# Seven quarter products from chunk 4 on, and a row's scores and values in different chunks

## The chip, the cores and the metric

The kernel runs on one core of a Trainium2 chip. The time is device time in microseconds of one launch, from the median of several runs. TensorE is PE in the views, and its weight loads PEld; VectorE is DVE, ScalarE is ACT, GpSimd is POOL, SyncE is SP. A "q" behind a name (SPq, POOLq) means that engine's queue of DMA issues and waits.

## What is computed

Local attention in two kinds of heads, and behind it a two-layer network on all tokens:

```python
# q, k, v: (8 batches, 8 heads, 576, 64) float32; w_in (512, 2048), w_out (2048, 512)
scores = q @ k.T / 8
# heads 0-3: key in the last 32 positions; heads 4-7: every 4th of the last 128
attn = softmax(where(mask, scores, -1e9))
x = (attn @ v).transpose(0, 2, 1, 3).reshape(4608, 512)
out = maximum(x @ w_in, 0) ** 2 @ w_out
```

The 4608 x 512 result is float32. Inside, the kernel works in float16 and accumulates in float32 in PSUM.

## The kernel before

**Two units.** A *row* is one batch: 576 tokens of attention. A *chunk* is 512 tokens of the network (chunk 0 takes row 0's 576 tokens whole, chunk 1 then has 448). So eight rows feed nine chunks: row b is wanted by chunk b and lies beside chunk b-1 in the program.

**The network.** The first product of a chunk (`mm1_gen`, L285, L264) makes sixteen tiles of 128 hidden units by 512 tokens, with four 512-wide matmuls each. ACT applies the relu from PSUM into `rt` (L249); DVE squares it into `g` (L253). The plain second product (`mm2_gen`, L316, L296) has four tiles of 16 matmuls, 512 wide. Chunks 7 and 8 use a Winograd form instead (`seven_gen`, L408, L401): `g` and `w_out` are cut into 2 x 2 quarters, DVE forms sums of quarters (`sum_g`, L372, for S1 to S4; `sum_w_out`, L359, for T1 to T4), PE makes seven products of quarters with 16 matmuls each, 256 wide, and DVE combines them from PSUM (L446 to L472).

**Attention of a row.** Four score groups (`s_sliding`, L582, twice, and `s_dilated`, L589, twice): PE writes scores into a pair of PSUM banks, ACT takes the exponential into `AT` (L547), DVE multiplies with a 0/1 mask (L549). Then seven groups of values (`av_sliding`, L609, three; `av_dilated`, L624, four): PE multiplies `AT` with `v` and its column of ones, DVE takes the reciprocal of the sum and multiplies (L600, L601). Last come four groups of PE transposes (`x_sliding`, L638; `x_dilated`, L655), which ACT copies into `xT` (L650, L668). `xT` is a ring of four rows; a chunk whose tokens cross the ring's end has each matmul of its first product cut in two (`cut`, L260).

**What sets the order.** Each engine works through its instructions in the order in which the program emits them. The network's generators yield after every half tile of the first product (two matmuls), every two matmuls of the second and every four of the seven, and `pump(n)` (L486) lets them go n steps: the first product has 32 steps, the plain second product 32, the seven 28 in all. Before, each chunk ran 24 steps, then four score groups 4 steps apart, then values and transposes 2 steps apart (L673, L681, L892 on). PSUM has eight banks: four for the network (`bank`), and two pairs for attention (`pair`).

**Loads.** POOL waits with a one-element copy (`see`, L181) until row b's q and k have landed, then issues the loads of row b+1's, copies these into token order (L225) and casts row b's v (L197, L201). SP issues, in this order within a chunk, the DMA transposes of row b+1 into `QKTd` and `QKTp` (two buffers each), the loads of its v, and the chunk's stores.

Of the kernel before, what the change touches and what calls it, by code (L numbers as in the profile page):

```python
# [8 lines left out]
FP16 = mybir.dt.float16  # L9
FP32 = mybir.dt.float32  # L10
# [3 lines left out]
P = 128  # L14
# [3 lines left out]
def kernel(  # L18
# [40 lines left out]
    natp = ctx.enter_context(tc.tile_pool(name="natp", bufs=2))  # L59
# [27 lines left out]
    RING = 4 * S  # L87
# [8 lines left out]
    g = wpool.tile([P, NFF, S], FP16, name="g")  # L96

# [149 lines left out]
    def relu_squared(ph, w, outs, name):  # L247
        rt = osb.tile([P, TOKC], FP16, name=name, tag="rt")
        nc.scalar.activation(rt[:, 0:w], ph[:, 0:w], ACTF.Relu)  # L249
        o = 0  # L250
        for g in outs:
            n = g.shape[1]
            nc.vector.tensor_mul(g, rt[:, o : o + n], rt[:, o : o + n])  # L253
            o += n

    def mm1_tile(name, ffc, t0, t1, outs):
# [16 lines left out]
        relu_squared(ph, w, outs, f"rt{name}")  # L273
        yield

    def mm1_first_gen():

        for f4 in range(0, NFF, 4):
            for t0 in (0, HALF):
                for ffc in range(f4, f4 + 4):  # L280
                    yield from mm1_tile(
                        f"0_{ffc}_{t0}", ffc, t0, t0 + HALF, [g[:, ffc, t0 : t0 + HALF]]
                    )

    def mm1_gen(c, then=None):  # L285
        o = REST if c == 1 else 0
        for ffc in range(NFF):
            yield from mm1_tile(
                f"{c}_{ffc}", ffc, c * TOKC + o, (c + 1) * TOKC, [g[:, ffc, o:TOKC]]
            )  # L290
            if then is not None:
                then(ffc)
# [50 lines left out]
    sums = {}  # L343

    def quarters():

        for i, tag in enumerate(("nd", "nd", "n", "n", "o", "o")):
            shape = {"nd": [P, 36 * D], "n": [P, HH, 9, D], "o": [P, 9, HH, D]}[tag]
            u = natp.tile(shape, FP16, name=f"sum{i}", tag=tag)
            if tag != "nd":  # L350
                u = u.rearrange("p a b d -> p (a b d)")
            sums[("T1", "T2", "T3", "S1", "S2", "S3")[i]] = u[:, 0 : HF * HT].rearrange(
                "p (j t) -> p j t", j=HF
            )
        u = sd.rearrange("p t h x -> p (t h x)").bitcast(FP16)
        for i, name in enumerate(("T4", "S4")):
            sums[name] = u[:, HF * HT * i : HF * HT * (i + 1)].rearrange("p (j t) -> p j t", j=HF)

    def sum_w_out(name, j):  # L359

        f = slice(4 * j, 4 * j + 4)
        b11, b12 = wo[j][:, :, 0:HT], wo[j][:, :, HT:DM]
        b21, b22 = wo[2 + j][:, :, 0:HT], wo[2 + j][:, :, HT:DM]
        a, b = {
            "T1": (b12, b11),
            "T3": (b22, b12),
            "T2": (b22, sums["T1"][:, f, :]),
            "T4": (b21, sums["T2"][:, f, :]),
        }[name]
        nc.vector.tensor_sub(sums[name][:, f, :], a, b)  # L370

    def sum_g(name, j):  # L372

        f, h = slice(4 * j, 4 * j + 4), slice(HF + 4 * j, HF + 4 * j + 4)
        a11, a12 = g[:, f, 0:HT], g[:, h, 0:HT]
        a21, a22 = g[:, f, HT:TOKC], g[:, h, HT:TOKC]
        o = sums[name][:, f, :]
        if name == "S1":
            nc.vector.tensor_add(o, a21, a22)
        elif name == "S3":  # L380
            nc.vector.tensor_sub(o, a11, a21)
        elif name == "S2":
            nc.vector.tensor_sub(o, sums["S1"][:, f, :], a11)
        else:
            nc.vector.tensor_sub(o, a12, sums["S2"][:, f, :])

    def sums_behind(ffc):
        for name, j in {
            8: (("S3", 0),),
            9: (("S3", 1),),  # L390
            12: (("S1", 0),),
            13: (("S2", 0),),
            14: (("S4", 0),),
            15: (("S1", 1), ("S2", 1), ("S4", 1)),
        }.get(ffc, ()):
            sum_g(name, j)

    def product(po, lhs, rhs):
        for t in range(2):
# [6 lines left out]
            yield  # L406

    def seven_gen(c):  # L408
# [6 lines left out]
        def s(name):  # L415
            return lambda j: sums[name][:, j, :]

        def new(name):
            return osb.tile([P, 2, HT], FP32, name=f"{name}{c}", tag=name, bufs=1)
# [8 lines left out]
        def keep(i, k, o):  # L428
            for t in range(2):
                nc.sync.dma_start(out=rows(i, k, t), in_=o[:, t, :])  # L430
# [5 lines left out]

        p1, po = one()
        yield from product(po, a(0, 0), b(0, 0))
        s1 = new("s1")
        nc.scalar.copy(s1, p1)  # L440
        p7, po = one()
        yield from product(po, s("S3"), s("T3"))
        p2, po = one()
        yield from product(po, a(0, 1), b(1, 0))
        c11 = outcome("c11")
        nc.vector.tensor_add(c11, p2, s1)  # L446
        keep(0, 0, c11)
        p6, po = one()
        yield from product(po, s("S2"), s("T2"))
        u2, t7 = new("u2"), new("t7")  # L450
        nc.vector.tensor_add(u2, p6, s1)
        nc.vector.tensor_add(t7, p7, u2)
        p5, po = one()
# [92 lines left out]
    def softmax(u, ps, mask, eng=nc.vector):  # L546
        nc.scalar.activation(AT[:, u, 0:UW], ps[:, :, 0 : UW // 2], ACTF.Exp, scale=scale)  # L547
        if mask is not None:
            eng.tensor_mul(AT[:, u, 0:UW], AT[:, u, 0:UW], mask)  # L549
# [397 lines left out]
```

## Time and profile before

| what | us |
|---|---|
| median of 3 runs (lowest, highest) | 314.33 (313.9, 314.9) |
| the profiled execution | 315.87 |
| its span, from the first to the last instruction | 313.8 |
| PE busy in the span | 299.6 |
| DVE, ACT, POOL busy | 181.7, 167.3, 78.0 |
| first products (L264), 704 matmuls, on the chain that ended last | 39.0% |
| plain second products (L296), 448 matmuls, on that chain | 30.3% |
| seven products (L401), 224 matmuls, on that chain | 7.8% |

The span covers what the profiler recorded of the program; the execution's own time has 2.1 us more around it. Durations are those of one execution. A matmul's recorded duration is longer than the distance to the next one, since matmuls are pipelined, so PE's rate is read from the distance between starts or from the chain's merged pieces, where "x64" stands for that many instructions in a row.

### The profile page before, as it was taken

How to read it: one execution, taken by the hardware profiler on the slowest of the kernel's cores; microseconds unless marked ns; L12 is line 12 of the kernel's file. 1: busy time of each engine (PE TensorE's matmuls, PEld its weight loads, DVE VectorE, ACT ScalarE, POOL GpSimd, SP SyncE). 2: the span in 40 equal slices, each digit the busy share in tenths (PEclk: the TensorE clock that was granted, in tenths of full speed). 3: DMA queues.
4: the chain of work that ended last, by engine and by line, in shares of the span. 5: the costliest groups of instructions: out<-in, count | busy, mean ns of one | idle time of the engine just before them, and what ended most of it. 6: DMA issues, size and time to landing. Idle time of an engine off the chain costs nothing.

```text
span 313.8 us, 6835 instructions
## 1 busy us (share of the span) xinstructions
PE 299.6 (96%) x2724; PEld 183.7 (59%) x2724; DVE 181.7 (58%) x402; ACT 167.3 (53%) x295; POOL 78.0 (25%) x120
## 2 busy tenths in 40 slices
PE   3978999999899999999999999999999999999995
PEld 3647955555455555555579655545554555686584
DVE  6445647736742795396524653475388534854764
ACT  2646856378336753677257724683368336604610
POOL 5483016403523633263340370032000000000000
PEclk9989999999999999999999999999999999999999
DMA  6999989599989999998968992992100110012012
GB/s 118 223 191 214 212 179 216 123 164 256 229 185 202 278 193 188 236 280 172 221 218 193 176 239 75 186 206 101 45 25 1 41 61 36 1 40 96 0 36 100
DMA packets 73951, 46.71 MB, mean 149 GB/s; under 512 B 54528, under 2 KB 68096, under 8 KB 73728
## 3 DMA queue, kind: packets, MB, share of 16 engines
q1 hardware_dynamic: 66384, 32.39, 43.2%
q0 software_dynamic: 7248, 13.63, 24.4%
q8 instruction: 21, 0.34, 0.4%
q10 hardware_dynamic: 288, 0.26, 0.2%
q14 instruction: 10, 0.08, 0.1%
HBM read 39.85 MB, written 16.52 MB: 180 GB/s over the span
## 4 chain that ended last, share of the span: by engine, by line
PE 88%; DMA 7%; POOL 2%; issue 1%; ACT 1%; DVE 0%; POOLq 0%
PE PS L264 39%; PE PS L296 30%; PE PS L401 8%; PE PS L629 3%; DMA wi<-in_moe_w_in_dram 3%; DMA sd<-in_v_dram 2%; DMA n<-in_q_dram 2%; PE PS L615 2%; PE PS L574 1%; PE PS L644 1%; PE PS L560 1%; PE PS L662 1%; ACT AT L547 0%; PE PS L504 0%; PE PS L528 0%
## 5 line engine op out<-in xcount | busy, mean ns | idle before, releaser
L264 PE MATMUL PS<-xT,wi 128*128 128x512 f16 (+3 forms) x704 | 130.3, 343 | 1.8 <-DMA wi<-in_moe_w_in_dram 1.1
L249 ACT ACTIVATE rt<-PS 128x512 f16<-128x512 f32 (+2 forms) x160 | 88.8, 556 | 44.6 <-PE PS L264 40.5
L296 PE MATMUL PS<-wo,g 128*128 128x512 f16 x448 | 112.5, 379 | 0.0
L253 DVE TENSOR_TENSOR g<-rt 128x512 f16<-128x512 f16 (+2 forms) x160 | 69.8, 443 | 72.1 <-ACT rt L249 71.5
L264 PEld LDWEIGHTS <-wi 128*128 128x128 f16 x704 | 78.4, 114 | 46.8 <-DMA wi<-in_moe_w_in_dram 1.2
L296 PEld LDWEIGHTS <-g 128*128 128x128 f16 x448 | 37.3, 97 | 31.4
L547 ACT ACTIVATE AT<-PS 128x576 f16<-128x576 f32 x64 | 38.3, 650 | 8.6 <-PE PS L574 5.7
L306 ACT COPY ot<-PS 128x512 f32<-128x512 f32 x28 | 16.4, 586 | 28.8 <-PE PS L296 28.8
L650 ACT COPY xT<-PS 128x576 f16<-128x576 f16 x16 | 10.2, 639 | 29.4 <-PE PS L644 29.4
L201 POOL CAST vd<-sd 128x512 f16<-128x512 f32 x32 | 20.5, 669 | 14.7 <-DMA sd<-in_v_dram 12.5
L197 POOL CAST vp<-sv 128x512 f16<-128x512 f32 x24 | 16.7, 710 | 27.1 <-DMA sv<-in_v_dram 27.1
L601 DVE TENSOR_TENSOR x_d<-PS,rcp_d 72x512 f16<-72x512 f32 x32 | 22.0, 686 | 1.1
L225 POOL COPY o<-n 128x2304 f16<-128x2304 f16 x6 | 12.6, 2107 | 27.8 <-DMA n<-in_q_dram 27.6
L549 DVE TENSOR_TENSOR AT<-AT,maskd 128x576 f16<-128x576 f16 x28 | 14.6, 539 | 7.0 <-ACT AT L547 5.6
L600 DVE RECIPROCAL rcp_d<-PS 72x8 f32<-72x8 f32 x32 | 6.5, 202 | 20.7 <-PE PS L629 19.6
L629 PEld LDWEIGHTS <-AT 128*128 128x128 f16 x256 | 12.8, 102 | 7.8 <-DVE x_d L601 0.8
L601 DVE TENSOR_TENSOR x_p<-PS,rcp_p 96x512 f16<-96x512 f32 x24 | 16.5, 686 | 0.8
L549 DVE TENSOR_TENSOR AT<-AT,maskp 128x576 f16<-128x576 f16 x28 | 14.3, 524 | 4.0 <-ACT AT L547 2.1
L668 ACT COPY xT<-PS 128x576 f16<-128x576 f16 x16 | 10.2, 640 | 8.8 <-PE PS L662 8.8
L629 PE MATMUL PS<-vd,AT 128*128 128x65 f16 x256 | 14.3, 200 | 0.0
L183 POOL COPY look<-QKTp 1x1 f16<-1x1 f16 x5 | 1.2, 239 | 49.3 <-DMA QKTp<-dp 49.3
L615 PEld LDWEIGHTS <-AT 128*128 128x128 f16 x192 | 9.2, 99 | 6.6 <-issue 1.2
(86 smaller groups left out, 207.9 us busy)
## 6 DMA issues: line engine op xcount, KB each, us to landing
out_dram<-ot SPq DMA_DIRECT2D x27, 256.0 KB, 2.8
sv<-in_v_dram SPq DMA_DIRECT2D x40, 128.0 KB, 4.6
sd<-in_v_dram SPq DMA_DIRECT2D x8, 512.0 KB, 11.4
dp<-o SPq DMA_DIRECT2D x12, 288.0 KB, 3.7
sd<-in_v_dram SPq DMA_DIRECT2D x8, 288.0 KB
wo<-in_moe_w_out_dram POOLq DMA_DIRECT2D x4, 512.0 KB, 13.6
out_dram<-c SPq DMA_DIRECT2D x14, 128.0 KB, 1.8
n<-in_k_dram POOLq DMA_DIRECT2D x6, 288.0 KB, 6.1
```

Source lines behind the costliest of these rows:

```text
L197: nc.gpsimd.tensor_copy(vp[b % 2][:, m : m + 2, :, 0:D], sv[:, m : m + 2, :, :])
L201: nc.gpsimd.tensor_copy(vd[b % 2][:, t, c : c + 2, :, 0:D], sd[:, t, :, D * c : D * (c + 2)].rearrange("p h (c d) -> p c h d", d=D),)
L249: nc.scalar.activation(rt[:, 0:w], ph[:, 0:w], ACTF.Relu)
L253: nc.vector.tensor_mul(g, rt[:, o : o + n], rt[:, o : o + n])
L264: nc.tensor.matmul(ph[:, a:b], w_in_of(dmk, ffc), xT[:, dmk, x : x + b - a], start=(dmk == 0 and a == 0), stop=(dmk == NDM - 1 and b == w),)
L296: nc.tensor.matmul(po, g[:, ffc, o + t * P : o + (t + 1) * P], w_out_of(ffc), start=(ffc == 0), stop=(ffc == NFF - 1),)
L306: nc.scalar.copy(ot, po)
L401: nc.tensor.matmul(po[t], lhs(j)[:, t * P : (t + 1) * P], rhs(j), start=j == 0, stop=j == HF - 1)
L547: nc.scalar.activation(AT[:, u, 0:UW], ps[:, :, 0 : UW // 2], ACTF.Exp, scale=scale)
L549: eng.tensor_mul(AT[:, u, 0:UW], AT[:, u, 0:UW], mask)
L601: nc.vector.tensor_tensor(out=x[0:w], in0=pv[:, :, :, 0:D], in1=rcp[0:w].unsqueeze(3).to_broadcast([w, 2, HH, D]), op=ALU.mult,)
L629: nc.tensor.matmul(pav[:, e, h * (D + 2) : h * (D + 2) + D + 1], AT[:, 4 + 2 * a + t, off : off + P], vd[b % 2][:, t, 2 * a + e, h, 0 : D ...
```

## The change

- Chunks 4, 5 and 6 use the seven products as well. The sums of `w_out` are made once, in chunk 2. S4 takes S3's place after product 7, and its two sums come behind product 2.
- Rows 2 and 3 keep their places. Row 4 has its scores at steps 2 to 20 of chunk 3 and its values at 24 to 44; row 5 its scores at 47 to 59 of chunk 3 and its values in the first half of chunk 4; rows 6 and 7 have their scores at steps 36 to 54 of chunks 4 and 5, their values at steps 2 to 32 of the chunk after. From row 4 on the transposes use the pair banks too (`wide`).
- Squares are made for two tiles in one DVE instruction, masks for two tiles likewise. A quarter of the result is stored by one DMA.
- The ring `xT` has three rows; `n` and `o` have one buffer each; S1 to S3 and T4 have tiles of their own; the first rows' staging tiles share slots with T1 to T3.
- In the seven, product 4 skips the bank of product 7.

The diff, cut to its core:

```diff
-    natp = ctx.enter_context(tc.tile_pool(name="natp", bufs=2))
+    n1p = ctx.enter_context(tc.tile_pool(name="n1p", bufs=1))
+    natp = ctx.enter_context(tc.tile_pool(name="natp", bufs=1))
...
-    RING = 4 * S
+    RING = 3 * S
...
+    S1, S2, S3 = (wpool.tile([P, NFF // 2, TOKC // 2], FP16, name=f"S{i}") for i in (1, 2, 3))
+    T4 = wpool.tile([P, NFF // 2, TOKC // 2], FP16, name="T4")
...
-        relu_squared(ph, w, outs, f"rt{name}")
-        yield
+        nc.scalar.activation(rt, ph[:, 0:w], ACTF.Relu)
+
+    def new_rt(name):
+        return osb.tile([P, 2, TOKC], FP16, name=f"rt{name}", tag="rt", bufs=3)
...
+        for f2 in range(0, NFF, 2):
+            rt = new_rt(f"{c}_{f2}")
+            for i in range(2):
+                yield from mm1_tile(f2 + i, c * TOKC + o, (c + 1) * TOKC, rt[:, i, o:TOKC])
+                if i == 1:
+                    nc.vector.tensor_mul(g[:, f2 : f2 + 2, o:TOKC], rt[:, :, o:TOKC], rt[:, :, o:TOKC])
+                    if then is not None:
+                        then(f2)
+                yield
...
+    def sum_g(name, j):
+
         f = slice(4 * j, 4 * j + 4)
+        if name == "S3":
+            nc.vector.tensor_sub(S3[:, f, :], a_of(0, 0, j), a_of(1, 0, j))
+        elif name == "S1":
+            nc.vector.tensor_add(S1[:, f, :], a_of(1, 0, j), a_of(1, 1, j))
         elif name == "S2":
+            nc.vector.tensor_sub(S2[:, f, :], S1[:, f, :], a_of(0, 0, j))
         else:
+            nc.vector.tensor_sub(S3[:, f, :], a_of(0, 1, j), S2[:, f, :])
+
+    def sums_behind(f2):
         for name, j in {
             8: (("S3", 0),),
+            10: (("S3", 1),),
+            12: (("S1", 0), ("S2", 0)),
+            14: (("S1", 1), ("S2", 1)),
+        }.get(f2, ()):
             sum_g(name, j)
...
         def keep(i, k, o):
-            for t in range(2):
-                nc.sync.dma_start(out=rows(i, k, t), in_=o[:, t, :])
+            t0 = c * TOKC + HT * i
+            nc.sync.dma_start(
+                out=out[t0 : t0 + HT, HT * k : HT * (k + 1)].rearrange("(t p) m -> p t m", p=P),
+                in_=o,
+            )
...
         yield from product(po, a(0, 1), b(1, 0))
+        for j in range(2):
+            sum_g("S4", j)
         c11 = outcome("c11")
...
+        turn["bank"] += 1
         p4, po = one()
...
+    def softmax(u, tiles, mask):
+
+        n = len(tiles)
+        for i, ps in enumerate(tiles):
+            nc.scalar.activation(
+                AT[:, u + i, 0:UW], ps[:, :, 0 : UW // 2], ACTF.Exp, scale=scale
+            )
         if mask is not None:
+            nc.vector.tensor_mul(
+                AT[:, u : u + n, 0:UW],
+                AT[:, u : u + n, 0:UW],
+                mask.unsqueeze(1).to_broadcast([P, n, UW]),
+            )
...
-        t0 = (b % 4) * S + 288 * half
+        t0 = (b % 3) * S + 288 * half
...
+    def run(*plans, more=()):
+
+
+        todo = list(more)
+        for plan, parts in plans:
+            for w in plan.split():
+                step, *names = w.split(":")
+                todo += [(int(step), parts[n]) for n in names]
+        at = 0
+        for step, part in sorted(todo, key=lambda t: t[0]):
+            pump(step - at)
+            at = max(at, step)
+            part()
+        pump(1000)
...
+    rows_ = {b: row_parts(b, b > 3) for b in range(2, B)}
+    SCORES = "{}:s0 {}:s1 {}:z0 {}:z1"
+    VALUES = "{}:a0 {}:a1 {}:a2 {}:x0 {}:d0 {}:x1 {}:d1 {}:e0 {}:e1 {}:y0 {}:y1"
+    for c in range(1, NTOKC):
+        b = c + 1
...
+        pending.append(moe_gen(c) if c < 4 else moe_seven_gen(c))
+        plans, more = [], []
+        if c < 3:
+            plans.append((SCORES.format(*range(24, 40, 4)), rows_[b]))
+            plans.append((VALUES.format(*range(40, 62, 2)), rows_[b]))
+        if c == 2:
+            it = sum_w_out_gen()
+            more = [(4 + 7 * i, lambda it=it: next(it)) for i in range(8)]
+        if c == 3:
+            plans.append((SCORES.format(2, 8, 14, 20), rows_[b]))
+            plans.append((VALUES.format(*range(24, 46, 2)), rows_[b]))
+            plans.append((SCORES.format(47, 51, 55, 59), rows_[b + 1]))
+        if 3 < c < B - 1:
+            plans.append((VALUES.format(2, 5, 8, 11, 13, 16, 18, 22, 26, 29, 32), rows_[b]))
+        if 3 < c < B - 2:
+            plans.append((SCORES.format(36, 42, 48, 54), rows_[b + 1]))
+        run(*plans, more=more)
```

In the plans, a0 to a2 are the value groups of the plain heads, d0, d1, e0 and e1 those of the dilated heads, x0, x1, y0 and y1 the transposes, s0, s1, z0 and z1 the score groups.

## The prediction

> **What bounds the kernel now.** I read the page's busy times first, then the chain that ended last in order of time, then one table with a row for each chunk, then the engines' timelines around the places that the change moves work to.
>
> ```profile
> PE 299.6 (96%) x2724; PEld 183.7 (59%) x2724; DVE 181.7 (58%) x402; ACT 167.3 (53%) x295; POOL 78.0 (25%) x120
> ...
> PE 88%; DMA 7%; POOL 2%; issue 1%; ACT 1%; DVE 0%; POOLq 0%
> ```
> ```profile
> 258.12 13.81 PE PS L264 x64
> 271.93 12.23 PE PS L401 x112
> ```
> ```profile
> 193.39:225.75 32.36, 32.36 (x270) 17.18 (x268) 17.06 (x38) 18.68 (x32) 4.69 (x7) 1.00 0.58 137
> ...
> 258.12:284.16 26.04, 26.04 (x177) 18.23 (x176) 15.92 (x31) 10.73 (x18) 0.00 (x0) 1.00 0.10 33
> ```
>
> The first fence is the page, the second the chain by time (start, length), the third the table by chunk. The chain is TensorE's. The table's rows (stretch, length, busy PE, PEld, DVE, ACT, POOL, clock) show chunks 5 and 7: PE fills them, its clock whole. So a chunk lasts as long as its PE instructions take: a first product is 64 x 215.8 ns = 13.81 us, a plain second product of 64 like matmuls the same, seven quarter products 112 x 109.2 ns = 12.23 us. What is left of chunk 5, 32.36 - 27.62 = 4.74 us, is one row's attention: four score groups of 0.36 or 0.37, seven value groups and four transposes of 0.26 (4.3 us by the chain's pitches) and 0.4 us of changing over.
>
> **What is removed.** Chunks 4, 5 and 6 change from the plain second product to the seven: 3 x (13.81 - 12.23) = **-4.74 us**. Moving a row's attention between chunks doesn't change its PE time; it counts only where something makes PE wait. On PE I find two additions.
>
> (1) **The ring.** With 3 rows of 576 tokens, chunks 3 (at 192 of 512) and 6 (at 384) cross its end; now only chunk 4 does. That crossing costs 32.52 - 32.37 = 0.15 us: 64 more matmuls, pieces of 256 at 109.2 ns against 215.8 whole, so 2.6 ns each plus 0.416 a column. Two crossings in place of one: **+0.15 us**, if a piece of 128 (55.9 ns) still hides the weight load of its follower. In a stream, no row shows loads from `wi` (every fourth column) closer than 109 ns, chunk 4's pace: the upper bound. Lower: the value groups do 8 matmuls, each with its own contiguous weights, in 0.26 us, 33 ns each, and two `wi` loads at 24.55 began 40 ns apart (0.15 us for two records of 0.11). The records are 113 ns long for `wi`, 98 for contiguous weights; 15 more on 33 is an estimate of 48 ns, which I take as the nearest to both rows. Were it 109, pieces of 128 and 192 (82.6 ns) would cost 64 x (53 + 26) ns = 5.1 us: that end is a rival below.
>
> The Trainium skill has a rule that speaks against this step: "TensorE: Matmul & The Clock Gate", section "LDWEIGHTS (loading the stationary operand)", gives a load of 128 columns as 128/1.2 = 107 ns. The 33 ns row contradicts it for contiguous weights; by the page the two crossings would cost 64 x (51 + 24) ns = 4.8 us, and the whole sum would be about +1.3 us.
>
> (2) **Waits for DVE**, whose order is fixed by the program. Its prices:
>
> ```profile
> 266.56 0.42 DVE L253 TENSOR_TENSOR g<-rt 128x512 f16<-128x512 f16 x1 [0.44 <-ACT rt L249]
> 266.90 0.69 DVE L381 TENSOR_TENSOR sum<-g 128x1024 f16<-128x1024 f16 x1
> 267.50 0.42 DVE L253 TENSOR_TENSOR g<-rt 128x512 f16<-128x512 f16 x1
> ```
> ```profile
> 185.21 0.69 DVE L601 TENSOR_TENSOR x_d<-PS,rcp_d 72x512 f16<-72x512 f32 x1
> ```
> ```profile
> 131.76 1.81 DVE L253 TENSOR_TENSOR g<-rt 128x512 f16<-128x512 f16 x1 [0.44 <-ACT rt L249]
> ```
> ```profile
> 131.16 2.12 POOL L225 COPY o<-n 128x2304 f16<-128x2304 f16 x1 [6.46 <-DMA n<-in_q_dram]
> ```
>
> Starts, then lengths: behind each other a square of 512 holds DVE 0.34 us, a sum of 1024 0.60. A paired square has the sum's shape and type, so 0.60 for two in place of 0.68. From both sides: 0.60, or 1.2 if it ran like the f32 adds (0.69 for 512); same type as the f16 sum, I take 0.60. A paired mask of 1152 is 0.69 + 128 x 0.52 ns = 0.75 by the same slope, 1.4 at the f32 rate; its repeated operand costs nothing in the row where the masks are made (L737, 459 ns for 576, both inputs repeated, against 458 for L549). The last two lines show that a DVE operation on two SBUF inputs stands still while POOL copies: the square took 1.81. Beside POOL's casts squares and casts alternate at 0.75 us (7 of them after 133.5), so about 0.41 more each. The normalising product reads PSUM and SBUF, and is 0.69 throughout.
>
> Chunks 4 to 6, first half: 8 squares (4.8), 7 normalisations of 0.85 (5.9), 6 sums (3.7): 14.4 us of DVE in 13.81 + 11 x 0.26 = 16.7 us of PE. Second half: 2 sums, 7 adds of 0.69, 4 masks: 8.8 in 12.23 + 1.46 = 13.7. It fits; what counts is order. Laid out by step (0.43 us), a2's normalisation waits behind the square of step 8 and ends about 6.35 us into the chunk; d0, which takes over a2's PSUM pair, is due at 6.66. Other links have 0.5 us or more. S2 is ready 2.6 us after the first half, its product starts 5.6 us after it. So chunks 5 and 6: nothing. If DVE were 0.3 us later, each of the links a2-d0, d0-d1, d1-e1, e1-y1 would begin to cost.
>
> Chunk 4 also has POOL's copy and casts for row 6 in its second half (181.7 to 190): masks and the two S4 sums wait 0.41 each, so the add c11 ends about 10.5 us after the first half; product 4 needs its bank at 10.1. **+0.4 us**. Chunk 3 has row 4's scores beside POOL's casts and then row 4's values two steps apart, all on pair banks; a0's normalisation starts 1.2 us late, and a2, d0, d1 each lose 0.1 to 0.2: **+0.4 us**. In chunks 1 and 2 the longer DVE operations hold POOL's casts up 0.3 us more where PE already waits for a cast (0.92 us in chunk 1, "PE PS L615 <- POOL vp L197"): **+0.3 us**, between -0.9 (that wait gone) and +0.7.
>
> **At no cost.** ACT: chunk 3's first half has 16 relus and 8 exponentials of some 0.6, 14.4 us in 16.3. The sums of `wo` (8 x 0.60) move from chunk 6 to 2, where DVE is busy 19.7 of 32.4 us; behind them comes the last square, wanted 3 us into the second product. Larger stores: half the issues on SP; no store is waited for. T4 and the S tiles on their own: no row shows a wait for their old places.
>
> **Queues.** Scores earlier need q and k earlier:
>
> ```profile
> 161.95 2.79 SPq L243 DMA_TRANSPOSE QKTd<-dd  x2
> ...
> 168.32 2.70 SPq L239 DMA_TRANSPOSE QKTp<-dp  x2
> ```
> ```profile
> 173.12 0.48 POOL L183 COPY look<-QKTp 1x1 f16<-1x1 f16 x1 [11.85 <-DMA QKTp<-dp]
> ```
>
> SP stands behind the stores of the chunk in front, so row 6's transposes start when chunk 4 does (160.87) and have landed 12.3 us later. Its scores now come at step 36 of chunk 4: 13.81 + 2.9 + 1.75 = 18.4 us in. Margin 6 us; row 7 in chunk 5 likewise (transposes from 194.5, landed about 206); row 5 landed at 146.1, wanted at about 152; row 4 at 121.9, wanted at 129. Values: row 5 wants its first casts at 163, they are done at 158; row 6 at 194, done by 188.5, some 1.5 later in the new order. All hidden; past the margins PE would wait one for one.
>
> **Sum:** -4.74 + 0.15 + 0.4 + 0.4 + 0.3 = **-3.5 us**. The profiled execution was 315.87 (span 313.8 and 2.1 around it), so about 312.4 by it; the median of the runs, 314.33, is 1.5 lower and gives **310.8**.
>
> **Rivals.**
> - *DVE becomes the bound of the first halves* of chunks 3 to 6: four links each 0.2 us late in three chunks and 1 us in chunk 3 more: +3.4 at most, 312 to 314.2. For it: 14.4 of 16.7 us and one engine order; against: the order laid out above fits.
> - *Weight loads pace the short pieces*: up to +5.1, so 315.9; from 97 ns a load the gain is gone. Against: the rows of 33 and 40 ns.
> - *The first product waits for the copies into the ring* (the slower side). Four transposes of a row now lie among matmuls that read other rows of the same `xT`. If those wait for the copy, as at 27.31 where PE stood 0.73 us for "ACT xT L650" (there truly needed), 14 copies (12 in chunks 4 to 6, 2 in chunk 3) cost 0.73 to 1.1 each: 10 to 15 us, 321 to 326. It decides from 5 such waits on. For it: no row of before has such a copy beside unrelated reads. Against: engines read one slice of `PS` and write another at once all through the trace.
> - *The rows' data come late*, the change not doing what it says: above 6 us of slip, 312 to 316. Against: the landings above.
>
> **Numbers.** Forecast 0.62 (309.7 to 311.9); DVE 0.18; weight loads 0.06; ring copies 0.08; late rows 0.06. A measurement here tells 0.3%, 0.94 us, from no change: faster is below 313.4, slower above 315.3. Faster: 0.62 + 0.12 + 0.02 = 0.76. Same: 0.05 + 0.03 + 0.02 = 0.10. Slower: 0.01 + 0.03 + 0.08 + 0.02 = 0.14. The range: 309.2 (chunk 1's wait half gone, no DVE waits) to 314.1 (DVE's case whole) leaves out the ring copies and halves of two others, 0.16.
>
> **What would show it.** Stretches of 112 matmuls in chunks 4 to 6, which last about 30.8, 30.8 and 29.4 us (the last without scores) with PE busy throughout; chunk 3 about 34 (row 5's 1.46 us of scores added). No "PE PS L264 <- ACT xT" in the list of waits; paired squares at 0.69, masks at 0.75; `QKTp` landing before its score group. Wrong if PE stands before L264 in the first halves, if groups of values wait for `rcp` or `x` by more than a microsecond in sum, or if chunks 3 and 6 show a first product longer than 14.1 us without attention.

## The result, and the profile after

The changed kernel takes **312.15 us** (median of 20 runs, 311.34 to 314.29) against 314.88 for the kernel before (20 runs beside it, 313.82 to 317.28): ratio 0.9916, 95% interval 0.9896 to 0.9936. It is faster by 2.73 us; the forecast was 3.5. Both profiled executions, 315.87 before and 313.25 after, are about 1 us above their kernel's median. The profiled execution after is 2.62 us shorter than that of before; its span is 311.2.

The page after, first busy times, then the shares of the chain that ended last:

```profile
PE 297.2 (95%) x2932; PEld 200.7 (65%) x2932; DVE 198.2 (64%) x354; ACT 161.8 (52%) x286; POOL 85.4 (27%) x120
...
PE 92%; DVE 2%; DMA 2%; ACT 2%; issue 1%; POOL 0%; DVEq 0%; POOLq 0%
```

PE is still the bound, with 2.4 us less to do. The chain in order of time has a stretch of 112 matmuls in chunk 6 now, as long as those of chunks 7 and 8:

```profile
243.31 12.23 PE PS L396 x112
255.54 13.81 PE PS L260 x64
```

The table by chunk (stretch, length, busy PE, PEld, DVE, ACT, POOL, clock, DMA), chunks 3 to 6:

```profile
128.50:163.30 34.80, 34.80 (x390) 23.21 (x389) 20.19 (x30) 22.80 (x40) 18.47 (x21) 1.00 0.85 196
163.30:194.72 31.42, 30.91 (x318) 21.73 (x317) 24.42 (x40) 17.63 (x30) 9.38 (x13) 1.00 0.78 170
194.72:226.40 31.68, 30.95 (x319) 21.84 (x317) 24.02 (x41) 17.04 (x29) 5.43 (x7) 1.00 0.61 140
226.40:255.45 29.05, 29.05 (x326) 24.62 (x325) 20.98 (x37) 12.28 (x21) 0.00 (x0) 1.00 0.11 38
```

In chunks 3 and 6 PE is busy throughout; in 4 and 5 it is not: 0.51 and 0.73 us are missing. That is the first finding. VectorE, the busiest beside PE, has 24.4 us in 31.4. Its prices, and GpSimd's copy beside it:

```profile
184.24 1.84 DVE L573 TENSOR_TENSOR AT<-AT,maskp 128x1152 f16<-128x1152 f16 x1 [0.95 <-ACT AT L569]
...
205.94 0.69 DVE L294 TENSOR_TENSOR g<-rt 128x1024 f16<-128x1024 f16 x1 [0.57 <-ACT rt L269]
```
```profile
183.36 2.10 POOL L230 COPY o<-n 128x2304 f16<-128x2304 f16 x1 [4.83 <-issue]
```

A paired square is 0.69 long, as the sum of its shape was; a paired mask is 0.76 when alone, and 1.84 beside the copy. Row 6's transposes and GpSimd's look at them:

```profile
170.93 2.76 SPq L244 DMA_TRANSPOSE QKTp<-dp  x2
```
```profile
175.78 0.18 POOL L188 COPY look<-QKTp 1x1 f16<-1x1 f16 x1 [15.87 <-DMA QKTp<-dp]
```

They are in by 175.8, and the scores that read them start at 182.42, a margin of 6.6 us where 6 was forecast. In chunks 3 to 6 PE's list of waits has no wait for a load: no row's data came late.

Where the time went, from the start of each chunk's first product to the next one's, in one profile of each kernel:

| stretch | before | after | difference |
|---|---|---|---|
| up to chunk 0's second product | 41.03 | 40.70 | -0.33 |
| chunk 0's second product, with row 1 beside it | 23.20 | 24.75 | +1.55 |
| chunk 1 | 31.74 | 30.65 | -1.09 |
| chunk 2 | 32.37 | 32.37 | 0 |
| chunk 3 | 32.36 | 34.80 | +2.44 |
| chunk 4 | 32.53 | 31.43 | -1.10 |
| chunk 5 | 32.36 | 31.65 | -0.71 |
| chunk 6 | 32.36 | 29.04 | -3.32 |
| chunks 7 and 8, end | | | 0 |

They sum to -2.56; the spans, 313.8 and 311.2, differ by 2.6.

### The profile page after: what moved, and what is told of

The parts are those of the page before. It is cut to its first block, busy times and chain, and to the rows that moved or that the text cites. A ratio compares the mean times of both kernels' runs of the same rounds, so it can differ in the third digit from the quotient of the medians.

```text
span 311.2 us, 7133 instructions
## 1 busy us (share of the span) xinstructions
PE 297.2 (95%) x2932; PEld 200.7 (65%) x2932; DVE 198.2 (64%) x354; ACT 161.8 (52%) x286; POOL 85.4 (27%) x120
## 3 DMA queue, kind: packets, MB, share of 16 engines
q1 hardware_dynamic: 67952, 32.52, 44.4%
## 4 chain that ended last, share of the span: by engine, by line
PE 92%; DVE 2%; DMA 2%; ACT 2%; issue 1%; POOL 0%; DVEq 0%; POOLq 0%
PE PS L260 41%; PE PS L396 20%; PE PS L301 17%; PE PS L655 3%; PE PS L588 2%; PE PS L641 2%; PE PS L602 2%; DMA nd<-in_q_dram 2%; PE PS L688 1%; PE PS L670 1%; PE PS L523 1%; DVE AT L573 1%; ACT AT L569 1%; PE PS L581 1%; DVE x_p L627 1%
## 5 line engine op out<-in xcount | busy, mean ns | idle before, releaser
L260 PE MATMUL PS<-xT,wi 128*128 128x512 f16 (+6 forms) x768 | 136.1, 329 | 2.9 <-ACT xT L676 1.7
L294 DVE TENSOR_TENSOR g<-rt 128x1024 f16<-128x1024 f16 (+1 forms) x64 | 47.6, 747 | 38.5 <-ACT rt L269 38.4
L301 PE MATMUL PS<-wo,g 128*128 128x512 f16 x256 | 64.4, 379 | 0.0
L396 PEld LDWEIGHTS <-S 128*128 128x128 f16 x320 | 31.0, 98 | 3.8
L396 PE MATMUL PS<-T,S 128*128 128x256 f16 x240 | 28.2, 273 | 0.0
L573 DVE TENSOR_TENSOR AT<-AT,maskp 128x1152 f16<-128x1152 f16 x14 | 15.0, 1072 | 19.1 <-ACT AT L569 19.1
L206 POOL CAST vd<-sd 128x512 f16<-128x512 f32 x32 | 23.7, 773 | 10.5 <-DMA sd<-in_v_dram 10.4
L396 PE MATMUL PS<-wo,g 128*128 128x256 f16 x160 | 19.5, 273 | 0.0
L676 ACT COPY xT<-PS 128x576 f16<-128x576 f16 x16 | 10.2, 637 | 14.6 <-PE PS L670 14.5
L573 DVE TENSOR_TENSOR AT<-AT,maskd 128x1152 f16<-128x1152 f16 x14 | 12.8, 917 | 7.3 <-ACT AT L569 7.3
L283 DVE TENSOR_TENSOR g<-rt 128x288 f16<-128x288 f16 x32 | 9.9, 309 | 9.9 <-ACT rt L269 9.8
```

Of the source, the lines that this page charges most:

```text
L206: nc.gpsimd.tensor_copy(vd[b % 2][:, t, c : c + 2, :, 0:D], sd[:, t, :, D * c : D * (c + 2)].rearrange("p h (c d) -> p c h d", d=D),)
L260: nc.tensor.matmul(ph[:, a:b], w_in_of(dmk, ffc), xT[:, dmk, x : x + b - a], start=(dmk == 0 and a == 0), stop=(dmk == NDM - 1 and b == w),)
L294: nc.vector.tensor_mul(g[:, f2 : f2 + 2, o:TOKC], rt[:, :, o:TOKC], rt[:, :, o:TOKC])
L301: nc.tensor.matmul(po, g[:, ffc, o + t * P : o + (t + 1) * P], w_out_of(ffc), start=(ffc == 0), stop=(ffc == NFF - 1),)
L396: nc.tensor.matmul(po[t], lhs(j)[:, t * P : (t + 1) * P], rhs(j), start=j == 0, stop=j == HF - 1)
L573: nc.vector.tensor_mul(AT[:, u : u + n, 0:UW], AT[:, u : u + n, 0:UW], mask.unsqueeze(1).to_broadcast([P, n, UW]),)
```

## The experiments

Stretches in the text are measured like those of the table, each from one profile of the kernel named. Medians are given beside the ratio to the kernel before, run on the same chip in the same set. There were three sets; the changed kernel was measured again in the first and in the third, since sets differ by more than some of the effects sought. "The stage of row 1" is chunk 0's second product, which has row 1's attention beside it.

### The changed kernel again

> The changed kernel once more, beside the three below. Its waits are the subject of this series: in the profile after, PE stood before the first product until the copy of the transposes y0 had ended, 0.68 us in chunk 4 and 0.89 us in chunk 5, and not in chunk 6; and in chunk 0 the value group a2 came 1.09 us late, because the paired mask of z1 stood 2.27 us beside POOL's copy (53.62 to 55.73). Theory: the first two waits are fixed by the program and come again in the same two chunks with 0.7 to 0.9 us each; the third depends on when row 2's loads land and may be absent. Rival: all three come and go with the loads. Ratio to before 0.990 to 0.993.

313.26 us (8 runs), ratio 0.9947 (0.992 to 0.9974). The ratio is above the 0.990 to 0.993 that were expected. Chunks 3 to 6 last 34.79, 31.52, 31.64 and 29.05: the same waits in chunks 4 and 5 to 0.1 us. But chunk 0's second product lasts 23.46 in place of 24.75. So the two waits belong to the program, and the loss in row 1's stage comes and goes. The waits, in the profile of the changed kernel (PE in chunk 4, ACT in chunk 4, PE in chunk 5):

```profile
178.34 0.38 PE L260 MATMUL PS<-xT,wi 128*128 128x512 f16 x1
179.24 1.24 PE L260 MATMUL PS<-xT,wi 128*128 128x512 f16 x5 [0.51 <-ACT xT L694]
```
```profile
178.55 0.64 ACT L694 COPY xT<-PS 128x576 f16<-128x576 f16 x1
```
```profile
210.66 1.46 PE L260 MATMUL PS<-xT,wi 128*128 128x512 f16 x6 [0.73 <-ACT xT L694]
```

The first product of chunk 4 reads row 3's and 4's tokens, and the copy of y0 writes row 5's: another part of `xT`. PE still stands until the copy ends (178.55 + 0.64 = 179.19) and goes on 0.05 us later. In chunks 3 to 6 ten copies into the ring have a first product's matmuls behind them: x0 in chunk 3, and x0, x1 and y0 in each of chunks 4 to 6. Two of the ten are waited for, y0 in chunk 4 and y0 in chunk 5.

### y0 three steps later

```diff
-            plans.append((VALUES.format(2, 5, 8, 11, 13, 16, 18, 22, 26, 29, 32), rows_[b]))
+            plans.append((VALUES.format(2, 5, 8, 11, 13, 16, 18, 22, 26, 32, 32), rows_[b]))
```

> Only the place of y0 changes: from step 29, between the halves of the first product's tile 14, to step 32, behind its last matmul, in chunks 4 to 6. Theory (the first product's matmul behind y0 waits for y0's copy into another row of the ring): with no first product behind it the two waits go, 1.5 us less than the changed kernel, chunks 4 and 5 about 30.8 us, ratio to before about 0.987. Rival (the copy only seemed to release PE, and PE waited for an engine or a PSUM bank that is late at that place anyway): the wait moves to the seven products, gain under 0.3 us. Risk on both: y0 and y1 then lie together, and the pair banks are wanted again at step 36, 1.75 us later, while two copies take about 1.2 us.

311.71 us (6 runs), ratio 0.9912 (0.9878 to 0.9945). Behind the last matmul that reads `xT`, y0's copy is waited for by nobody: chunks 4 and 5 last 30.76 each. That is 0.67 and 0.89 less than in the first profile after, 1.56 together. The waits shown are 1.24: idle time is counted from the end of the record in front, and a record runs some 0.16 us beyond the usual start of the next matmul (0.38 long, for a distance of 0.216). By medians the kernel is 1.55 under the changed one of its set, with intervals that overlap; the chunk lengths carry the finding. In chunk 1, where nothing was changed, a wait for a cast of v was there:

```profile
82.94 0.42 PE L641 MATMUL PS<-vp,AT 128*128 128x65 f16 x8 [1.66 <-POOL vp L202]
```

### y0's copy in two, in its old place

```diff
-        nc.scalar.copy(
-            xT[:, 2:4, t0 : t0 + 288].rearrange("x c (i r) -> x c i r", r=DIL),
-            py[:, 0:UW].rearrange("x (c r i) -> x c i r", c=2, r=DIL),
-        )
+        for c in range(2):
+            nc.scalar.copy(
+                xT[:, 2 + c, t0 : t0 + 288].rearrange("x (i r) -> x i r", r=DIL),
+                py[:, 288 * c : 288 * (c + 1)].rearrange("x (r i) -> x i r", r=DIL),
+            )
```

> y0 and y1 keep their steps; each one's copy into the ring is made as two copies, one for each 128 columns of x, so that one instruction writes one stretch of 288 tokens and not two stretches a ring's length apart. Everything else is the changed kernel. Theory (the wait comes from the two stretches written by one instruction, between which the next reads lie): both waits go although nothing runs earlier, 1.3 to 1.5 us less than the changed kernel, against some 0.15 us of ACT for each of 16 more instructions off the path. Rival (PE really needs ACT at that place): the waits stay, and are 0.1 to 0.2 us longer.

311.49 us (6 runs), ratio 0.9905 (0.9872 to 0.9938). Its table for chunks 4 and 5, and PE behind y0 in chunk 4:

```profile
162.87:193.63 30.76, 30.76 (x318) 21.74 (x317) 25.08 (x40) 17.66 (x32) 11.89 (x16) 1.00 0.80 170
193.63:224.39 30.76, 30.76 (x319) 21.74 (x317) 25.17 (x42) 17.07 (x31) 6.48 (x7) 1.00 0.71 148
```
```profile
177.96 1.46 PE L260 MATMUL PS<-xT,wi 128*128 128x512 f16 x6
```

The copy is in the same place, on the same engine, and nothing waits. So PE did not need ScalarE there for anything else: the wait belongs to y0's copy as one instruction, and with two instructions of one stretch each it is gone. The data do not need it, since the copy and the matmul touch different parts of `xT`.

Which property of the one instruction makes the wait is not shown. It writes two stretches of 288 tokens, 1728 apart in each partition, and the two matmuls that waited are the first whose read lies between them: in chunk 4 the one on the fourth 128 channels of x, in chunk 5 already the one on the third. But that is not enough for a wait. The copies of x0 and x1 (L676) write two such stretches too, and in chunk 4 PE goes on before x1's copy has begun, with the read of the second 128 channels, at 171.92, between its stretches (PE, then ACT):

```profile
171.70 1.03 PE L260 MATMUL PS<-xT,wi 128*128 128x512 f16 x4
```
```profile
172.14 0.63 ACT L676 COPY xT<-PS 128x576 f16<-128x576 f16 x1
```

And in chunk 6, y0's copy has the form that it has in chunks 4 and 5, again with reads between its stretches, and PE runs through it:

```profile
241.57 1.48 PE L260 MATMUL PS<-xT,wi 128*128 128x384 f16 x12
```
```profile
241.77 0.64 ACT L694 COPY xT<-PS 128x576 f16<-128x576 f16 x1
```

So two stretches with reads between them are not enough. The pattern of y0's write has groups of four tokens within each stretch besides (the copy brings the dilated tokens back into order), which x0's and x1's has not; the edit leaves the groups and takes the two stretches apart. No run separates these properties, and none says why chunk 6 is spared.

Chunk 3 lasted 35.55 in this profile, with a wait of 0.75 for row 4's normalisation at a2: a paired mask took 2.58 us there (133.21 to 135.79), with GpSimd's copy running from 133.07 to 135.18.

### Row 1's masks one by one again

```diff
+            if mask is not None and single["on"]:
+                nc.vector.tensor_mul(AT[:, u + i, 0:UW], AT[:, u + i, 0:UW], mask)
-        if mask is not None:
+        if mask is not None and not single["on"]:
```

> Only row 1's masks, in chunk 0's second product, go back to one DVE instruction for each tile, as in the kernel before; rows 2 to 7 keep the paired masks. In the profile after, that stage took 24.75 us against 23.20 before, and chunk 1 30.65 against 31.74. Theory (a paired mask waits for both exponentials, so it holds the copies of the next transposes 0.2 to 0.3 us each, and when POOL's copy begins first it holds a2 a microsecond more; part of it is given back in chunk 1, whose values before waited 0.92 us for a cast): the stage 0.5 to 1.5 us shorter, the sum of stage and chunk 1 0.3 to 0.6 us shorter, ratio to before about 0.990. Rival (pairing costs nothing and the difference is when the loads landed): the stage still about 24.7 us in some profiles, no gain beyond 0.1 us.

312.74 us (12 runs), ratio 0.9931 (0.9909 to 0.9954). The stage of row 1 lasted 27.29, longer than with paired masks. DVE, POOL and PE of this kernel:

```profile
51.14 5.89 DVE L575 TENSOR_TENSOR AT<-AT,maskd 128x576 f16<-128x576 f16 x4 [0.87 <-ACT AT L571]
```
```profile
54.33 2.39 POOL L230 COPY o<-n 128x2304 f16<-128x2304 f16 x1 [0.26 <-DMA n<-in_q_dram]
```
```profile
57.92 0.27 PE L645 MATMUL PS<-vp,AT 128*128 128x65 f16 x3 [2.71 <-DVE x_p L631]
```

Four masks, 0.46 us each when alone, take 5.89, with GpSimd casting v from 51.56 on and copying from 54.33; a0's normalisation is queued behind them on VectorE, and a2 takes over a0's banks. The same in the profile of the changed kernel (DVE, POOL, PE), and DVE in the changed kernel's second profile:

```profile
54.07 2.27 DVE L573 TENSOR_TENSOR AT<-AT,maskd 128x1152 f16<-128x1152 f16 x1 [0.94 <-ACT AT L569]
```
```profile
53.62 2.11 POOL L230 COPY o<-n 128x2304 f16<-128x2304 f16 x1 [1.22 <-DMA n<-in_q_dram]
```
```profile
57.23 0.43 PE L641 MATMUL PS<-vp,AT 128*128 128x65 f16 x8 [1.09 <-DVE x_p L627]
```
```profile
53.57 0.76 DVE L573 TENSOR_TENSOR AT<-AT,maskd 128x1152 f16<-128x1152 f16 x1 [0.65 <-ACT AT L569]
```

In the second profile the copy starts at 54.42, when the mask is through. So the stage can be long without the pairing, and short with it. What goes with its length is where GpSimd's casts and copy fall, and these wait for loads (`sv`, `sd`, `n`). In before's profile the copy came at 56.62, the masks long done.

The Trainium skill says of this, in "SBUF — State Buffer", section "SBUF: two separate sides", that a VectorE operation with two SBUF inputs and a GpSimd operation that reads SBUF share a pair of ports, and that the one that starts first holds it for its whole instruction. The mask beside one copy agrees (2.27 for 0.76, the copy 2.11 long). Casts that follow each other at once can be harder on VectorE than that: in the kernel with y0's copy in two, one mask of row 1 took 2.73 us (51.15 to 53.88) while four casts went by, and the fifth then took 1.13 in place of 0.61.

### The copy into token order in four pieces

```diff
-        nc.gpsimd.tensor_copy(o, n.rearrange("p h j d -> p j h d"))
+        for h in range(HH):
+            nc.gpsimd.tensor_copy(o[:, :, h, :], n[:, h, :, :])
```

> The changed kernel with GpSimd's copy into token order in four pieces of 128x576 in place of one of 128x2304, in all rows. Theory (what takes 1 to 2.7 us in chunk 0's second product, and comes and goes, is one paired mask that stands still for the whole of that copy, 2.27 us in place of 0.76): a mask then waits for one piece at most, some 0.55 us, so a paired mask takes at most 1.4 us and the stage of row 1 lasts 23.3 to 24.2 us wherever the loads land. Rival (VectorE gets no turn between pieces that follow each other at once): a mask of 2 us and more, and a stage of 24.8 us when they meet. The time: 0 to 1.5 us under the changed kernel, 311.5 to 313.3.

311.98 us (10 runs), ratio 0.9915 (0.9893 to 0.9937). The stage lasted 23.96, in the range that the theory gave, but there the pieces (from 55.57) met only the end of a mask that took 1.16 us. The other took 2.19 (52.84 to 55.03) while three casts went by. In chunks 3 and 4 masks do meet the pieces, and VectorE gets its turn between them, as the theory said: in chunk 3 four pieces (131.85 to 136.02) take 0.89 to 1.19 each and the masks and squares among them 0.86 to 1.15, and in chunk 4 the mask that took 1.84 beside the whole copy takes

```profile
184.73 0.95 DVE L574 TENSOR_TENSOR AT<-AT,maskp 128x1152 f16<-128x1152 f16 x1 [0.95 <-ACT AT L570]
```

So in this profile the pieces shorten the longest stops. The time shows no gain by it (ratio 0.9915, the changed kernel's 0.9916), and chunk 3 lasted 35.08.

### Row 2's copy held back behind a2

```diff
+    def order_row_2():
+        see(parts["xs"][2][0:1, 0, 0, 0:1])
+        o = in_token_order(2, n)
+        transpose_dilated(2, dd)
+        transpose_sliding(2, keep_sliding_qk(2, o))
...
-            "... 20:a2 21:x0 ..."
+            "... 20:a2:o2 21:x0 ..."
```

> The changed kernel with row 2's copy into token order held back until a2 of row 1 is normalised. Theory (the loss in the stage of row 1 and the gain in chunk 1, whose wait for a cast of vp is gone, are one thing, GpSimd's chain running earlier): the stage lasts 23.2 to 23.6 us in the profile, no wait for x_p in it, masks of row 1 at most 1.1 us; the chain behind the copy starts 1 to 2 us later, and chunk 1 gets back a wait for vp of 0 to 1 us (30.7 to 31.6 us). The time: 311.5 to 313, between nothing and 1.5 us under the changed kernel. Rival (the stage is long because its masks are paired, or for its copies of QKTd): 24.5 us or more as in the changed kernel's profile.

312.46 us (10 runs), ratio 0.9939 (0.9907 to 0.9972). Its masks on DVE:

```profile
51.90 1.51 DVE L573 TENSOR_TENSOR AT<-AT,maskd 128x1152 f16<-128x1152 f16 x1 [1.11 <-ACT AT L569]
53.60 0.89 DVE L573 TENSOR_TENSOR AT<-AT,maskd 128x1152 f16<-128x1152 f16 x1 [0.19 <-ACT AT L569]
```

The stage is 23.54, without a wait of a2. One mask was longer than expected (1.51 against 1.1), beside two casts. Chunk 1 got no wait back (30.66). In the two kernels below, with the same edit, the stage is 23.58 and 23.54, where the changed kernel had 24.75, 23.46 and 24.26. That is not yet a proof that the edit keeps it short: of eight profiles with the copy where it was and the same masks, four have 23.46 or 23.47 and the others 24.26 to 25.16, so three short ones can be chance. The median shows no gain that the runs can tell.

### The plain second product in chunks 4 to 6

```diff
-        pending.append(moe_gen(c) if c < 4 else moe_seven_gen(c))
+        pending.append(moe_gen(c) if c < 7 else moe_seven_gen(c))
```

> The changed kernel with the plain second product (64 matmuls) in chunks 4 to 6 in place of the seven; all else, the order of the rows, the paired operations and the ring of 3, as changed. Theory (the seven are worth their full 1.58 us in each chunk, and the waits that were found lie in the first halves): +4.74 us on the changed kernel, about 317 to 318 us, so slower than the kernel before by some 2.5 us; the chunks 4, 5 and 6 last 33.0, 33.2 and 30.6 us. Rival (the seven lose part of their gain in their own halves, to the adds and S4 sums on VectorE): less than +4 us, chunks 4 to 6 under 32.6, 32.8 and 30.2.

318.29 us (4 runs), ratio 1.0113 (1.008 to 1.0146): slower than before. Chunks 4 and 6 in its table:

```profile
163.97:196.99 33.02, 32.51 (x270) 17.05 (x269) 15.87 (x26) 18.71 (x32) 10.10 (x13) 1.00 0.76 170
...
230.22:260.86 30.64, 30.64 (x278) 19.89 (x277) 11.32 (x22) 14.04 (x24) 0.00 (x0) 1.00 0.09 36
```

Against the first profile after, chunks 4, 5 and 6 (33.02, 33.23, 30.64) are 1.59, 1.58 and 1.60 longer, 4.77 together: the term at its full size. The waits for y0 are there too, so they have nothing to do with the seven. By its ratio the whole kernel lost more than 4.77, some 5 to 6 us; its profile has 0.35 more in chunk 3 and 0.42 more in the stage of row 1 as well. Without the seven the rest of the change is a loss.

### The rows where they were, seven products from chunk 4 on

```diff
-        if c < 3:
+        if c < B - 1:
             plans.append((SCORES.format(*range(24, 40, 4)), rows_[b]))
             plans.append((VALUES.format(*range(40, 62, 2)), rows_[b]))
...
-        if c == 3:
+        if c < 0:
...
-        if 3 < c < B - 1:
+        if c < 0:
...
-        if 3 < c < B - 2:
+        if c < 0:
```

> The changed kernel with the rows where they were before (a row's scores at steps 24 to 36 and its values at 40 to 60 of the chunk in front, for all chunks), seven products from chunk 4 on: the first part of the change without the second. TensorE's work is the same in sum. Theory (VectorE has no room in the second halves: 2 sums, 7 adds, 4 paired masks and 7 normalisations make 14.7 us, and the casts of GpSimd beside them 2 us more, in 17 us, in one order): waits for x, for rcp, for masks or for a product's bank of 1 to 2.5 us in each of the chunks 4 to 6, which last 32 to 33.5 us; the chunks 3 to 6 together 129 us against 126.9, the time some 2 us above the changed kernel. Rival (the move of the rows was not needed, it costs: the first product's waits for the copy of y0 go, and so do chunk 3's): chunks 4 to 6 at 30.8 to 31.2, chunk 3 at 32.4, together 125 to 126, the time 1 to 2 us under the changed kernel.

314.39 us (10 runs), ratio 0.9994 (0.9972 to 1.0017): as fast as before, so the medians show nothing of the seven's gain. Chunks 3 to 6 last 32.52, 31.61, 32.67 and 31.77, together 128.6 against 126.9 (129 was expected) and against 129.6 before: in these chunks 1 us of the 4.77 is left. The wait in its list:

```profile
PE PS L655 <- DVE x_p L627: 2.1, 3, 1.0
```

Once in each of chunks 4 to 6, d0 stands for a normalisation (0.53, 1.04 and 0.53): sums, masks, adds and normalisations are in one queue on VectorE in the second half. Each costs some 0.16 more than is shown, so the three are some 2.6 of the 3.5 us that chunks 4 to 6 take beyond a chunk without waits (30.8); the rest lies in smaller ones. This is the wait that the moved rows avoid, and it says that the two parts of the change need each other. Chunks 3 to 6 account for 1.7 us over the changed kernel, though row 1's stage was short in this profile (23.47).

### Squares one by one

```diff
-                    nc.vector.tensor_mul(g[:, f2 : f2 + 2, o:TOKC], rt[:, :, o:TOKC], rt[:, :, o:TOKC])
+                    for z in range(2):
+                        nc.vector.tensor_mul(g[:, f2 + z, o:TOKC], rt[:, z, o:TOKC], rt[:, z, o:TOKC])
```

> The changed kernel with the squares of chunks 1 to 7 made one by one again (two of 128x512 behind the second of a pair's relus, in place of one of 128x1024): the pairing of squares undone. Theory (VectorE had some 2 us to spare in the first halves, in the order laid out in the prediction): the first halves of chunks 4 to 6 hold 8 x 0.08 us more of VectorE, nothing or up to 0.3 us of waits a chunk, together under 1 us: 312 to 314. Rival of the prediction (VectorE is at the bound there): 0.6 us or more in each of chunks 3 to 6 and waits for x or rcp in the first halves, 315 or more.

313.86 us (10 runs), ratio 0.9927 (0.9892 to 0.9962); the changed kernel beside it had 0.9924. Chunks 3 to 6: 34.66, 31.94, 31.65 and 29.04. Chunks 3, 5 and 6 are as long as in the changed kernel or shorter, and the first halves show no wait for x or rcp, so VectorE was not at its bound there. Chunk 4 is 0.5 longer, by this:

```profile
189.90 1.03 PE L397 MATMUL PS<-T,g 128*128 128x256 f16 x8 [0.35 <-DVE c L451]
```

Product 4 waits for its bank: c11, the add that frees it, stands behind the two S4 sums, which took 2.10 beside GpSimd's casts. It is the wait that the prediction priced at 0.4 and that the changed kernel did not have (c11 ended at 190.05, the product started at 190.72). Whether the squares or the fall of the casts brought it about, one profile cannot tell.

### The changed kernel beside the mends

> The changed kernel once more, beside the next two on the same chip. 311.8 to 313.4 us; chunks 4 and 5 with the two waits of 0.5 to 0.7 us for the copy of y0; the stage of row 1 anywhere from 23.4 to 25 us, by where GpSimd's copy falls.

313.96 us (10 runs), ratio 0.9924 (0.9892 to 0.9956). The median is above the 311.8 to 313.4 that were expected. Chunks 4 and 5: 31.43 and 31.64, as expected; row 1's stage 24.26.

### Both mends, and a later row 4

The first has y0's and y1's copies in two and row 2's copy held back; the second has, besides,

```diff
-            plans.append((VALUES.format(*range(24, 46, 2)), rows_[b]))
-            plans.append((SCORES.format(47, 51, 55, 59), rows_[b + 1]))
+            plans.append((VALUES.format(*range(26, 48, 2)), rows_[b]))
+            plans.append((SCORES.format(48, 52, 56, 60), rows_[b + 1]))
```

> The changed kernel with the copies of y0 and y1 made in two (one for each 128 columns) and row 2's copy into token order held back behind a2 of row 1: two mends together. Theory: 1.54 us less from chunks 4 and 5 (30.77 each) and 0 to 1.3 us less from the stage of row 1 (23.5 in each profile): 310.3 to 311.5, about 0.5% under the changed kernel. Rival (what is taken from one wait is given back at the next): 312 or more, with a wait for vp in chunk 1 of a microsecond or more, or longer waits in chunk 3.

> As the kernel with both mends, and in chunk 3 row 4's values two steps later (26 to 46) and row 5's scores one step later (48 to 60). Theory (a2 and d1 of row 4 come 0.16 us too early each, because a0's normalisation waits behind the masks of z1): chunk 3 lasts 34.5 in place of 34.8 us, the time 0.3 us under the kernel with both mends. Rival (the lateness moves along: row 5's values in chunk 4 then wait for its masks): chunk 3 shorter, chunk 4 longer by as much.

311.56 us (6 runs), ratio 0.9874 (0.9832 to 0.9915), and 311.53 (6 runs), ratio 0.986 (0.9821 to 0.9898). Both medians are 2.4 under the changed kernel of their set, though the intervals still touch. Between the two there is no difference, where 0.3 was expected. The second one's table for chunks 3 to 6, and a line of its waits:

```profile
128.67:163.26 34.59, 34.59 (x390) 23.41 (x389) 22.29 (x30) 22.95 (x42) 19.46 (x21) 1.00 0.91 217
163.26:194.01 30.75, 30.75 (x317) 21.72 (x316) 25.13 (x41) 17.66 (x32) 9.30 (x13) 1.00 0.81 170
194.01:224.77 30.76, 30.76 (x318) 21.72 (x317) 25.18 (x42) 17.07 (x31) 6.65 (x7) 1.00 0.69 149
```
```profile
PE PS L641 <- POOL vp L202: 1.5, 1, 1.5
```

PE is busy without a gap in chunks 3 to 5 (the first kernel: 34.80, 30.85, 30.76). Chunk 3 lost 0.2 of its 0.4 us, and chunk 4 did not get it back. In chunk 1 the wait for a cast returned in the second kernel (chunk 1 32.29) and not in the first (30.66), with the same code there: GpSimd's look at row 2 came at 71.61 in the one and 69.71 in the other. All fourteen profiles fit this: chunk 1 lasts 30.65 to 30.76 where that look came at 69.71 or earlier, and 31.74 (before, 71.68), 32.48 (y0 later, 71.70) and 32.30 (this one) where it came later. Whether the held-back copy makes a late look likelier is open: one of three profiles with it has one, and one of ten changed kernels without it.

## Why the prediction was right, point by point

| step of the prediction | forecast | measured |
|---|---|---|
| seven products in chunks 4 to 6 | -4.74 | -4.77 (against plain ones) |
| ring crossed twice | +0.15 | +0.15 |
| waits for VectorE in chunk 3 | +0.4 | +0.4 (what is left of chunk 3; 0.3 is seen as late starts) |
| c11 late in chunk 4 | +0.4 | 0 |
| chunks 1 and 2, GpSimd's casts | +0.3 | -1.1 |
| y0's copies (a rival) | not in the sum | +1.56 |
| row 1's stage | not priced | +1.55 (0.3 and 1.1 in two others) |
| start | not priced | -0.3 |
| sum | -3.5 | -2.5; the spans differ by -2.6 |

**The seven products.** Right to 0.03 us: a duration from chunk 7's chain held three chunks earlier, with attention between.

**The ring, and the rival of weight loads.** Chunk 6's first product is 226.49 to 243.31 with eleven attention groups of 0.26: 16.82 - 2.86 = 13.96, so 0.15 over a whole one, with pieces of 384 and 128 columns. Pieces of 128 do hide the next weight load. The rule that the prediction quoted from the Trainium skill ("TensorE: Matmul & The Clock Gate", "LDWEIGHTS (loading the stationary operand)"), 107 ns a load, would have made it, by an estimate, 13.96 + 64 x 0.051 = 17.2 us; the measurement decides against it here. Two `wi` loads that the prediction read as 40 ns apart began 33 ns apart in the trace, so its estimate of 48 ns was on the safe side. Chunk 3 was forecast at 34, or 34.4 with its waits, and lasted 34.8: row 5's scores cost 1.84 with changing over (chunk 6 lost 1.87), not 1.46; that moves between chunks and sums to nothing.

**VectorE.** The prices of paired operations held (0.69 and 0.76), and so did the layout by step: a2 and d1 in chunk 3 were 0.15 and 0.16 late. The term for c11 was nothing: c11 ended 9.5 us after the first half, not 10.5, and product 4 started at 10.15. It was within the reach of GpSimd's casts, as the single squares show. The rival that VectorE bounds the first halves did not come true: 24.4 of 31.4 us, and no wait there even with 16 squares.

**The ring copies.** This rival was put as all or nothing, fourteen waits or none, and it happened at two. The count was too high to begin with: y1 in chunks 4 to 6 and x1 in chunk 3 have no first product behind them, which leaves ten. The step that failed is the argument against it, "engines read one slice of `PS` and write another at once": that says nothing of how a copy with another pattern is ordered against reads of its tile, and y0's was waited for in chunks 4 and 5. The price (0.73 to 1.1) was about right: 0.67 and 0.89. The prediction named "PE stands before L264 in the first halves" as a sign of being wrong, and this sign came.

**What was left out.** The step "at no cost" looked at chunks 2 to 6 only. The change emits paired masks in row 1's stage too, where before's trace already had casts beside masks, so it should have been priced, from nothing to the copy's 2.1 us. There a2 waited 1.09 us for a normalisation, which is the second sign of being wrong that the prediction named. Over all profiles with paired masks the stage is 0.3 to 2 us longer than before's 23.20, and where it is long, GpSimd's casts or copy stand beside the masks. Nor is the 1.1 us that chunk 1 saved shown to come from the change: its length goes with when GpSimd's look came, and two of the thirteen profiles of changed kernels have a chunk 1 longer than before's. Whether the kernel before has long stages of row 1, and short chunks 1, as often stays open: there is one profile of it.

**How far the number was luck.** The forecast was right in its sign and its main term, and too good by 0.8 us (medians) or 0.9 (profiles): +1.56 for y0 and +1.55 for row 1 were missing; 1.4 less than priced in chunk 1, 0.4 in chunk 4 and 0.3 at the start made up for most of it. So the main term was understood, but that the sum came so close is in good part luck: of 3.1 us that were missing 2.1 were given back elsewhere, 1.4 of it in chunk 1, whose length goes with when that look came. The median, 312.15, lies in the stated range of 309.2 to 314.1 but above the 309.7 to 311.9 of the forecast's own case, in the stretch that the prediction gave to the rival that VectorE bounds the first halves; by the number alone one would have believed that rival, and it needed the traces to see that it is not so. The kernel before took 314.88 in this set, not the 314.33 from which the forecast reckoned; from 314.88 the forecast would have been 311.4.

## What to carry to other kernels

When work moves to a place where others read the same tile, look in the trace at each instruction that writes it: it may be waited for by reads of other parts, and making it in two instructions can cost less than the wait. A product with fewer matmuls brings its whole gain only if the other engines' work for it is spread over both halves; without the second part of this change the medians showed no gain. And what depends on where a load lands should be read from several profiles: the stage of row 1 took 23.46 to 24.75 us in three runs of the same program, and chunk 1 took 30.66 and 32.30 in two kernels with the same code there. A sum whose parts miss in both directions can still come close; that is why each part is measured by itself.

## What the runs showed of the hardware

- A VectorE operation on two SBUF inputs can stand for several GpSimd casts that follow each other at once: in row 1's stage a mask of 0.76 us took 1.51 while two casts went by, 2.19 while three did and 2.73 while four did. It is not always so: in chunk 3 of the changed kernel casts (1.06 to 1.14 each) and squares (1.09 each) took turns one by one. What decides between the two is open.
- The matmul that waited for ScalarE's copy started 0.05 us after the copy's end. The wait shown as 0.51 us cost 0.67 in the chunk's length, and that of 0.73 cost 0.89, since a matmul's record ends some 0.16 us after the next one could have started.
- Matmuls of 384 and 128 columns in turn, each with its own load of 128 columns of weights, ran at 13.96 us for 64 pairs, against 13.81 for 64 of 512 columns, though each load's record is about 113 ns long and a piece of 128 columns lasts 55.9.
